# Attention and two feed-forward layers on one core: float32 products for the first pair of heads, one product for the last keys, and a new order

## The chip, the core and the metric

The kernel runs on one core of a Trainium2 chip. The core has five engines that run their own queues in order and wait for each other by semaphores: TensorE (PE in the profile; PEld is its loading of weights), VectorE (DVE), ScalarE (ACT), GpSimd (POOL) and SyncE (SP), which here only issues transfers. The metric is the device time of one execution in microseconds; lower is better. The kernel before took 784.59 us (median of three runs, 783.3 to 784.87).

## The reference, cut to what matters

Rotated attention over 2 batches of 8 heads, 576 tokens and 64 numbers a head; then a layer of four experts, all of which see every token, weighted by given shares; then a second feed-forward layer with a leaky rectifier.

```python
q_rot, k_rot = (rotate(q), rotate(k))       # x1*cos - x2*sin, x1*sin + x2*cos
scores = scale * np.matmul(q_rot, k_rot.transpose(0, 1, 3, 2))
scores = scores - np.max(scores, axis=-1, keepdims=True)
attn = np.exp(scores)
attn = attn / (np.sum(attn, axis=-1, keepdims=True) + 1e-09)
x = np.matmul(attn, v)                      # -> 1152 tokens x 512
...
for e in range(E):                          # 4 experts, 512 -> 1024 -> 512
    h = np.maximum(x @ w1[e], 0.0)
    out += p[:, e:e + 1] * (h @ w2[e])
...
h = x @ w_in                                # 512 -> 2048 -> 512
g = np.maximum(0.01 * h, h)
return g @ w_out
```

## The kernel before

Everything is float32 in and out. Most products are made of parts: a number is split into hi (rounded to the type fp32r) and lo (the rest), and a product becomes two to four products of parts. A split takes one instruction that rounds (`rounded`, on ScalarE or GpSimd) and one that subtracts.

**Attention** goes over eight pairs of heads, p = 0 to 7. For each pair q and k come in transposed, 128 rows (64 of either head) by 576 columns. They are rotated (`rope_mul` twice, `rope_add`; the names `x{p}_1` for k, `x{p}_0` for q), split (`x_hi`, `x_lo`) and stacked by transfers (`stk`), so that hi and lo of one head stand above each other. A pair has nine tiles of scores, numbered s0 to s71 over the whole kernel: four query blocks of 128 for each head, and one tile for the last 64 queries of both heads (576 = 4 x 128 + 64), whose weights lie in a block-diagonal tile `bd`. For each tile TensorE multiplies (`s_scores`), VectorE takes the negative maximum (`s_max`, tile `nm`), ScalarE the exponential (`s_exp`, tile `p`), TensorE turns the probabilities (`t_turn`, tile `t`), ScalarE and VectorE split what was turned (`t_hi`, `t_lo`, tile `pt`), and TensorE sums with v (`v_sum`, tile `o`). The keys are cut the same way; the last 64 keys of both heads share one tile of `pt`, and the tile `VZ` holds their v with zeros in the other head's rows. `v_sum` so takes ten products: four key tiles and the last keys, for lo and for hi of the probabilities. For pair 0 the split parts aren't stacked by transfers: q is copied into a zeroed `stk` (`first_zero`, `first_q`) and a tile of scores takes eight products of 288 columns; a later tile of 128 queries takes four.

**A part of the first layer lies in the attention.** As soon as the 512 tokens of block 0 are known (pairs 0 to 3), the three first half-experts are run for them in six steps v = 0 to 5 (`half_1`, tile `hp`; `half_2`, tile `hy`; VectorE's `half_relu` and `half_acc`): 288 products of 512 columns between the attention of pairs 4 to 7.

**The layers** then go over twelve units u of 512 hidden columns (eight of the first layer, four of the second) and three token blocks. For each unit the weights are loaded and split (`add_split`): in the first layer by GpSimd alone (L513 rounds, L517 subtracts, tiles `w` from `raw`), in the second, whose weights are 64-bit, by eight steps over VectorE, ScalarE and GpSimd (`split64`). `stage1` (L557, tile `ph`) and `stage2` (tile `py`) multiply.

**The order** of all this is made by a list planner (`Plan`): every task has engines that it may run on with a planned duration, tasks that it waits for, and a rank; the free engine takes the ready task of lowest rank. Ranks of the attention come from the tables `RANK` (three numbers a kind: first pair, pairs 1 to 3, pairs 4 to 7) and `MORE` (a penalty for the second engine). The planner fixes the order of every engine's queue; on the chip only semaphores decide when an instruction starts. Ahead of it, `WARM` products of the identity run on TensorE.

## Time and profile before

| | us |
|---|---|
| median of the runs | 784.59 |
| the profiled execution | 783.88 |
| its span, first to last instruction | 781.7 |
| TensorE busy | 756.2 (97%) |
| VectorE busy | 430.4 (55%) |
| GpSimd busy | 410.7 (53%) |
| ScalarE busy | 301.9 (39%) |

The shares are means over stages that differ. The span has four stretches: the start up to the first maximum, pairs 0 to 3, pairs 4 to 7 with the half-experts between them, and the layers. In each of them another engine can set the pace, so the rows below are read by stretch. "Granted clock" is the share of TensorE's full clock that the chip granted; 1.00 is the level of 2.4 GHz and 0.50 that of 1.2 GHz.

### The profile page before, as it was taken

The numbers are of one execution on the slowest core, as the hardware profiler recorded it, in microseconds if no ns is written. First come the engines' busy times: TensorE is split into PE (matmuls) and PEld (weight loads), VectorE is DVE, ScalarE is ACT, GpSimd is POOL, SyncE is SP. The second block draws the span as 40 slices with busy tenths as digits, with TensorE's granted clock in tenths as the row PEclk, the third lists the DMA queues.
The fourth block names the chain that finished last, engine by engine and source line by source line (L and its number), as shares of the span: only waits on it lengthen the run. The fifth ranks groups of instructions, "written<-read, shape, count | busy, mean of one in ns | idle before, by whom it ended". The sixth has DMA issues, their size and how long they took to land.

```text
span 781.7 us, 11049 instructions
## 1 busy us (share of the span) xinstructions
PE 756.2 (97%) x4204; PEld 667.0 (85%) x4204; DVE 430.4 (55%) x689; ACT 301.9 (39%) x686; POOL 410.7 (53%) x431
## 2 busy tenths in 40 slices
PE   6789899999999999999999999999999999999998
PEld 6778778888888989898898988988888889898897
DVE  7998977788752222232224222277668777762222
ACT  5688885766541111110112101143255454551221
POOL 7777857665339973433215331253157777782221
PEclk9999999999999999999999999999999999999999
DMA  7766545543053431320023100122113231000011
GB/s 254 184 194 158 148 109 141 169 118 100 24 220 108 136 104 37 102 55 30 25 54 105 58 28 28 54 84 80 55 55 107 61 103 55 0 1 1 1 55 67
DMA packets 31843, 67.70 MB, mean 87 GB/s; under 512 B 3888, under 2 KB 8752, under 8 KB 31792
## 3 DMA queue, kind: packets, MB, share of 16 engines
q1 hardware_dynamic: 30976, 66.22, 28.6%
q10 hardware_dynamic: 816, 0.79, 0.3%
q8 instruction: 33, 0.54, 0.3%
q14 instruction: 18, 0.15, 0.1%
HBM read 52.25 MB, written 2.36 MB: 70 GB/s over the span
## 4 chain that ended last, share of the span: by engine, by line
PE 84%; POOL 6%; DVE 5%; issue 2%; ACT 2%; DMA 1%; SPq 0%; POOLq 0%; DVEq 0%; ACTq 0%
PE py L463 33%; PE ph L557 32%; PE hp L660 4%; PE o L463 4%; PE hy L463 4%; PE s L303 4%; PE t L386 2%; POOL x L220 1%; DVE pt L415 1%; POOL x L223 1%; DVE nm L320 1%; DMA tab<-in_rope_dram 1%; DVE t L528 1%; ACT p L330 1%; POOL hw L653 1%
## 5 line engine op out<-in xcount | busy, mean ns | idle before, releaser
L557 PE MATMUL ph<-xT,w 128*128 128x256 f32 (+2 forms) x1584 | 276.0, 333 | 3.1 <-POOL w L517 1.6
L557 PEld LDWEIGHTS ph<-xT,w 128*128 128x128 f32 x1584 | 253.6, 190 | 23.0 <-POOL w L517 2.4
L463 PE MATMUL py<-w,h 128*128 128x512 f32 (+1 forms) x1164 | 268.0, 388 | 0.0
L463 PEld LDWEIGHTS py<-w,h 128*128 128x128 f32 x1164 | 215.8, 188 | 43.5
L564 ACT ACTIVATE h<-ph 128x384 fp32r<-128x384 f32 (+2 forms) x84 | 40.0, 476 | 249.2 <-PE ph L557 249.2
L568 DVE SCALAR_TENSOR_TENSOR h<-ph,h 128x384 fp32r<-128x384 f32 (+2 forms) x84 | 45.1, 537 | 114.3 <-ACT h L564 114.3
L513 POOL TENSOR_SCALAR w<-raw 128x512 fp32r<-128x512 f32 x64 | 38.5, 621 | 131.0 <-PE py L463 78.1
L603 DVE SCALAR_TENSOR_TENSOR acc<-py,prob,acc 128x512 f32<-128x512 f32 x55 | 41.2, 749 | 85.4 <-PE py L463 85.4
L582 POOL TENSOR_TENSOR h<-g,h 128x512 fp32r<-128x512 f32 (+2 forms) x48 | 52.1, 1086 | 63.4 <-ACT h L580 45.4
L517 POOL TENSOR_TENSOR w<-raw,w 128x512 fp32r<-128x512 f32 x64 | 81.2, 1291 | 0.0
L546 POOL TENSOR_TENSOR w<-t,w 128x512 fp32r<-128x512 f32 x32 | 44.5, 1403 | 53.2 <-ACT w L543 53.1
L415 DVE TENSOR_TENSOR pt<-t,pt 128x384 fp32r<-128x384 f32 (+2 forms) x128 | 60.0, 490 | 8.6 <-ACT pt L411 7.1
L303 PE MATMUL s<-stk 128*128 128x288 f32 x288 | 55.1, 323 | 8.9 <-ACT p L330 5.4
L411 ACT ACTIVATE pt<-t 128x384 fp32r<-128x384 f32 (+2 forms) x128 | 53.4, 439 | 24.2 <-PE t L386 20.8
L537 POOL TENSOR_TENSOR t<-t,r 128x512 int32<-128x512 int32 x32 | 44.4, 1388 | 26.2 <-DVE t L530 22.7
L330 ACT ACTIVATE p<-s,nm 128x576 f32<-128x576 f32 x72 | 53.2, 740 | 12.5 <-DVE nm L320 11.9
L320 DVE TENSOR_REDUCE nm<-s 128x1 f32<-128x576 f32 x72 | 53.6, 747 | 4.5 <-PE s L303 3.5
L303 PEld LDWEIGHTS s<-stk 128*128 128x128 f32 x288 | 43.6, 201 | 13.1 <-ACT p L330 7.8
L386 PE MATMUL t<-ident,p 128*128 128x128 f32 x288 | 46.2, 279 | 7.7 <-ACT p L330 3.4
L386 PEld LDWEIGHTS t<-ident,p 128*128 128x128 f32 x288 | 35.1, 142 | 14.3 <-ACT p L330 4.4
L463 PE MATMUL o<-pt,vs 128*128 128x320 f32 (+1 forms) x256 | 44.9, 302 | 0.1
L578 DVE TENSOR_TENSOR g<-ph,g 128x512 f32<-128x512 f32 (+2 forms) x48 | 26.4, 553 | 33.1 <-ACT g L576 33.1
(97 smaller groups left out, 837.5 us busy)
## 6 DMA issues: line engine op xcount, KB each, us to landing
raw<-in_w_dram SPq DMA_DIRECT2D x32, 512.0 KB, 3.7
raw<-in_w_in_dram SPq DMA_DIRECT2D x16, 512.0 KB, 3.8
raw<-in_w_out_dram SPq DMA_DIRECT2D x16, 512.0 KB, 3.6
x<-in_xqk_dram SPq DMA_DIRECT2D x14, 576.0 KB, 7.0
stk<-hl SPq DMA_DIRECT2D x28, 288.0 KB, 5.4
hraw<-in_w_dram SPq DMA_DIRECT2D x12, 512.0 KB, 3.8
stk<-hl SPq DMA_DIRECT2D x28, 144.0 KB, 3.3
v<-in_vp_dram SPq DMA_DIRECT2D x8, 288.0 KB, 4.7
```

Source lines behind the costliest of these rows:

```text
L303: pe.matmul(sc[:, c, :HS], lhsT=l, rhs=r[:, c * HS:(c + 1) * HS], start=(k == 0), stop=(k == len(ops) - 1))
L320: dve.tensor_reduce(out=NM[n], in_=SC[n][:, :, :HS], axis=AX.XY, op=ALU.max, negate=True)
L330: act.activation(PP[p, i][:, h].rearrange("p (c k) -> p c k", c=2), SC[n][:, :, :HS], AF.Exp, bias=NM[n], accum_out=SM[p][:, col:col + 1])
L386: pe.transpose(t[:, j], flat[:, b * P:(b + 1) * P], ident)
L411: act.activation(hi, src, AF.Copy)
L415: dve.tensor_tensor(out=lo, in0=src, in1=f32(hi), op=ALU.subtract)
L463: pe.matmul(ps, lhsT=l, rhs=r, start=(k == 0), stop=(k == len(ops) - 1))
L517: pool.tensor_tensor(out=w[:, 1], in0=raw, in1=f32(w[:, 0]), op=ALU.subtract)
L546: pool.tensor_tensor(out=w[:, 1], in0=f32(t), in1=f32(w[:, 0]), op=ALU.subtract)
L557: pe.matmul(ps, lhsT=w[:, c, l, fs], rhs=x[:, r, c], start=(c, k) == (0, 0), stop=(c, k) == (NC - 1, 2))
L568: dve.scalar_tensor_tensor(out=lo, in0=ps, scalar=0.0, in1=f32(hi), op0=ALU.max, op1=ALU.subtract)
L582: pool.tensor_tensor(out=lo, in0=g, in1=f32(hi), op=ALU.subtract)
```

## The change

- **First pair.** Its scores are made of two float32 products of 288 columns a tile; the parts, `x_hi`, `x_lo` and `first_q` are gone. The rotation of pair 0 runs on VectorE alone, with the scale in the product of q (`scalar_tensor_tensor`), and its sum writes straight into `stk` (`first_add`, for q one a head). The last queries of pair 0 use the tile `rr`.
- **Warm-up** of 28 products in place of 22. `fold` is gone: `r_rows` takes two float32 products with halves of the identity in place of one.
- **Last keys** of pairs 4 to 7 (`stacked`): for each head hi stands above lo in one block, so `v_sum` takes nine products in place of ten. For that the middle one of three turned tiles is split in three pieces (`t_hi`, `t_lo`: 256 columns, and twice 64 rows by 128).
- **First split** (unit 0): each rounding may go to ScalarE and each subtraction to VectorE.
- **Order**: other ranks for the first pair and for pairs 4 to 7 (the middle numbers stay), longer planned durations of `split64` and a rank 0.45 later, and a planned transfer rate of the first loads.

```diff
-WARM = 22
+WARM = 28
-RANK = {"tab_q": [2043.63, 1989.1, 2043.63], "zero": [1293.68, 1391.39, 1354.79], ...
+RANK = {"tab_q": [1899.26, 1989.1, 1475.09], "zero": [1519.84, 1391.39, 1696.99], ...
...
     def rope_mul(e, p, w, i, cs):
+        x = X[p, w][:, i, cs]
+        if p or w:
+            eng[e].tensor_tensor(out=x, in0=x, in1=(tab if w else tab_q)[:, i, cs], op=ALU.mult)
+        else:
+            dve.scalar_tensor_tensor(out=x, in0=x, scalar=SCALE, in1=tab[:, i, cs], op0=ALU.mult, op1=ALU.mult)
...
+    def first_k(cs=slice(0, S)):
+        return f32(stk_of(0)[:, 0, 1, cs])
+
+    def first_add(e, w, h, cs):
+        r = slice(64 * h, 64 * h + 64) if w == 0 else slice(0, P)
+        out = first_k(cs) if w else f32(stk_of(0)[r, h, 0, cs])
+        eng[e].tensor_tensor(out=out, in0=X[0, w][r, 0, cs], in1=X[0, w][r, 1, cs], op=ALU.add)
...
-        if p == 0 and i < KT:
-            ops = [(stk[:, h, a, at:at + P], k_of[b]) for a, b in ((1, 1), (0, 1), (1, 0), (0, 0))]
+        if p == 0:
+            ops = [(f32(stk[:, h, 0, at:at + P]) if i < KT else rr, first_k())]
...
-            pe.matmul(RB[p, c][:, 2 * P:], lhsT=rr, rhs=fold, start=True, stop=True)
+            products(RB[p, c][:, 2 * P:], [(rr, ident[:, :64]), (rr, ident[:, 64:])])
...
+        if i < KT and u == 1 and stacked(p):
+            if k == 0:
+                to, src = pt[:, :, 3:6:2, at:at + P], t[:, 0:3:2]
+            else:
+
+                h = k - 1
+                return pt[upper, h, KT, at:at + P], pt[lower, h, KT, at:at + P], t[64 * h:64 * h + 64, 1]
...
-            ops.append((VZ[p % 2][:, h].rearrange("p a d -> p (a d)"), pt[:, part, KT]))
+            if part == 0 or not stacked(p):
+                ops.append((VZ[p % 2][:, h].rearrange("p a d -> p (a d)"), pt[:, h if stacked(p) else part, KT]))
...
-                hi = plan.add(lambda e, c=c: split_hi(u, which, c), [("POOL", 0.6, 0)], loaded[c // 2:c // 2 + 1] + waits, rank + .1 * c)
+                hi = plan.add(lambda e, c=c: split_hi(e, u, which, c), [("POOL", 0.6, 0)] + [("ACT", 0.6, 0)] * (u == 0), loaded[c // 2:c // 2 + 1] + waits, rank + .1 * c)
...
-            for k, (e, us) in enumerate((("DVE", 0.4), ("DVE", 0.6), ("ACT", 0.55), ("ACT", 0.55), ("POOL", 1.2), ("DVE", 0.6), ("ACT", 0.5), ("POOL", 1.2))):
+            for k, (e, us) in enumerate((("DVE", 0.85), ("DVE", 1.0), ("ACT", 0.65), ("ACT", 0.65), ("POOL", 1.4), ("DVE", 1.0), ("ACT", 0.62), ("POOL", 1.38))):
...
-            split[u, which] = add_split(plan, u, which, loads, waits, rank, cv)
+            split[u, which] = add_split(plan, u, which, loads, waits, rank + (0.45 if u >= 2 * E else 0), cv)
```

What stands in the queues now, at three places. First VectorE at the start, up to the first maximum. Before (`x0_1` is k of pair 0, `x0_0` its q):

```order
L220 TENSOR_TENSOR x0_1_164<-x0_1_164,tab_132 128x288
L223 TENSOR_TENSOR x0_1_164<-x0_1_164 128x288
L244 TENSOR_TENSOR stk0_180<-x0_1_164,stk0_180 128x288
L220 TENSOR_TENSOR x0_1_164<-x0_1_164,tab_132 128x288
L220 TENSOR_TENSOR x0_0_178<-x0_0_178,tab_132 128x192
L223 TENSOR_TENSOR x0_1_164<-x0_1_164 128x288
L246 SCALAR_TENSOR_TENSOR hl0_208<-x0_0_178,hl0_208 128x192
L244 TENSOR_TENSOR stk0_180<-x0_1_164,stk0_180 128x288
L220 TENSOR_TENSOR x0_0_178<-x0_0_178,tab_132 128x384
L316 CAST bd0_135<-hl0_208 64x2x64
L220 TENSOR_TENSOR x0_0_178<-x0_0_178,tab_132 128x384
L320 TENSOR_REDUCE nm0_241<-s0_219 128x1
```

and after:

```order
L219 TENSOR_TENSOR x0_1_169<-x0_1_169,tab_131 128x288 x2
L234 TENSOR_TENSOR stk0_183<-x0_1_169 128x288
L219 TENSOR_TENSOR x0_1_169<-x0_1_169,tab_131 128x288
L221 SCALAR_TENSOR_TENSOR x0_0_181<-x0_0_181,tab_131 128x192 x2
L219 TENSOR_TENSOR x0_1_169<-x0_1_169,tab_131 128x288
L234 TENSOR_TENSOR stk0_183<-x0_0_181 64x192
L234 TENSOR_TENSOR stk0_183<-x0_1_169 128x288
L234 TENSOR_TENSOR stk0_183<-x0_0_181 64x192
L221 SCALAR_TENSOR_TENSOR x0_0_181<-x0_0_181,tab_131 128x384 x2
L335 TENSOR_REDUCE nm0_226<-s0_211 128x1
```

The three engines' chain of products, sum, rounding and subtraction has become products and sums on one engine; the copies into `bd` and the subtractions are gone from it.

Second, TensorE within pair 4, behind tile s40. Before (`hp` are products of the half-experts, `s` scores, `t` turns):

```order
L303 MATMUL s40_1516<-stk4_1202 128x288 x4
L660 MATMUL hp0_0_1524<-xT0_72,hw0_0_244 128x512 x3
L392 MATMUL t4_4_0_1532<-ident_64,p4_4_1501 128x64 x4
L393 MATMUL t4_4_0_1532<-ident_64,p4_4_1501 64x64
L660 MATMUL hp0_0_1524<-xT0_72,hw0_0_244 128x512 x3
L660 MATMUL hp0_1_1549<-xT0_72,hw0_0_244 128x512 x3
L392 MATMUL t4_4_1_1558<-ident_64,p4_4_1501 128x64 x4
L393 MATMUL t4_4_1_1558<-ident_64,p4_4_1501 64x64
L660 MATMUL hp0_0_1524<-xT0_72,hw0_0_244 128x512 x3
L386 MATMUL t4_1_0_1578<-ident_64,p4_1_1521 128x128 x3
```

and after:

```order
L319 MATMUL s40_1460<-stk4_1140 128x288 x4
L687 MATMUL hp0_0_1472<-xT0_71,hw0_0_217 128x512 x3
L407 MATMUL t4_4_0_1478<-ident_64,p4_4_1445 128x64 x4
L408 MATMUL t4_4_0_1478<-ident_64,p4_4_1445 64x64
L687 MATMUL hp0_0_1472<-xT0_71,hw0_0_217 128x512 x3
L407 MATMUL t4_4_1_1494<-ident_64,p4_4_1445 128x64 x4
L408 MATMUL t4_4_1_1494<-ident_64,p4_4_1445 64x64
L319 MATMUL s41_1503<-stk4_1140 128x288 x4
L687 MATMUL hp0_0_1472<-xT0_71,hw0_0_217 128x512 x3
L401 MATMUL t4_1_0_1520<-ident_64,p4_1_1484 128x128 x3
```

The next tile of scores stands ahead of products of the half-experts. Counted over the whole queue from s36 to s63 (pairs 4 to 6), 168 of the 288 products of the half-experts stood there before, and 120 now; the other 48 have gone behind s63. From s18 to s35 the order of TensorE is the same as before.

Third, where the layers begin: the split of unit 0 (`w0_0`), behind the last sum of the attention. GpSimd before:

```order
L458 TENSOR_TENSOR xT2_74<-xf7_1_2970,xT2_74 128x192
L513 TENSOR_SCALAR w0_0_3077<-raw0_0_0_3061 128x512 x2
L517 TENSOR_TENSOR w0_0_3077<-raw0_0_0_3061,w0_0_3077 128x512 x2
L513 TENSOR_SCALAR w0_0_3077<-raw0_0_1_3063 128x512 x2
L517 TENSOR_TENSOR w0_0_3077<-raw0_0_1_3063,w0_0_3077 128x512 x2
```

VectorE after, behind the last sum of the half-experts (two of the four subtractions; GpSimd keeps the other two and one rounding, ScalarE has three roundings):

```order
L712 SCALAR_TENSOR_TENSOR acc3_1841<-hy5_3_2992,prob_69,acc3_1841 128x512
L544 TENSOR_TENSOR w0_0_3063<-raw0_0_0_3047,w0_0_3063 128x512
L544 TENSOR_TENSOR w0_0_3063<-raw0_0_1_3049,w0_0_3063 128x512
```

The eight instructions of the split that were one queue are three queues now; VectorE's two stand behind `acc3`, which waits for the last product of the attention stage.

## Rows read from the trace of the kernel before

**Rows 1.** The page's first part: busy us, share of the span, instructions.

```profile
PE 756.2 (97%) x4204; PEld 667.0 (85%) x4204; DVE 430.4 (55%) x689; ACT 301.9 (39%) x686; POOL 410.7 (53%) x431
```

**Rows 2.** Busy time by stretch: stretch, length, engines, PEclk, DMA share, GB/s.

```profile
13.77:103.82 90.05, 76.96 (x540) 68.70 (x539) 81.41 (x156) 70.26 (x185) 72.06 (x79) 0.96 0.63 170
103.82:191.26 87.44, 86.52 (x547) 76.06 (x547) 67.72 (x123) 57.63 (x147) 56.23 (x69) 1.00 0.46 125
235.00:250.00 15.00, 13.23 (x59) 11.55 (x58) 4.00 (x7) 1.47 (x3) 15.00 (x18) 0.89 0.32 106
250.00:560.00 310.00, 310.00 (x1619) 273.91 (x1618) 111.97 (x168) 55.28 (x110) 126.95 (x131) 1.00 0.22 67
```

**Rows 3.** Timeline of the start, and s36's maximum: start, us, instruction, idle before it.

```profile
1.56 6.70 PE L698 MATMUL warm<-ident 128*128 128x128 f32 x44 [1.56 <-POOL ident masks.py:199]
4.75 0.46 DVE L220 TENSOR_TENSOR x<-x,tab 128x288 f32<-128x288 f32 x1 [0.39 <-DMA tab<-in_rope_dram]
...
7.48 1.33 DVE L220 TENSOR_TENSOR x<-x,tab 128x288 f32<-128x288 f32 x2 [0.16 <-DMA tab<-in_rope_dram]
...
11.53 3.89 PE L303 MATMUL s<-stk 128*128 128x288 f32 x16 [3.27 <-POOL vz L276]
...
13.77 0.76 DVE L320 TENSOR_REDUCE nm<-s 128x1 f32<-128x576 f32 x1
...
103.82 1.41 DVE L320 TENSOR_REDUCE nm<-s 128x1 f32<-128x576 f32 x2
```

**Rows 4.** Groups by shape: count | busy us, mean ns of one | idle before, releaser.

```profile
L246 DVE SCALAR_TENSOR_TENSOR hl<-x,hl 128x384 fp32r<-128x384 f32 x1 | 0.8, 819 | 0.0
...
L312 DVE CAST stk<-hl 64x768 fp32r<-64x768 f32 x1 | 0.9, 855 | 0.0
...
L316 DVE CAST bd<-hl 64x128 fp32r<-64x128 f32 x8 | 5.8, 731 | 0.1
...
L220 DVE TENSOR_TENSOR x<-x,tab_q 128x576 f32<-128x576 f32 x6 | 8.0, 1339 | 1.6 <-DMA x<-in_xqk_dram 1.6
...
L244 DVE TENSOR_TENSOR hl<-x,hl 128x576 fp32r<-128x576 f32 x7 | 6.9, 979 | 0.9 <-ACT hl L259 0.9
...
L223 DVE TENSOR_TENSOR x<-x 128x576 f32<-128x576 f32 x2 | 2.0, 994 | 0.1
...
L340 DVE TENSOR_SCALAR sm<-sm 128x4 f32<-128x4 f32 x3 | 1.7, 550 | 0.5 <-ACT p L330 0.5
...
L415 DVE TENSOR_TENSOR pt<-t,pt 128x384 fp32r<-128x384 f32 x96 | 51.0, 549 | 6.5 <-ACT pt L411 5.1
...
L415 DVE TENSOR_TENSOR pt<-t,pt 128x256 fp32r<-128x256 f32 x16 | 6.6, 415 | 2.0 <-ACT pt L411 1.9
...
L415 DVE TENSOR_TENSOR pt<-t,pt 64x64 fp32r<-64x64 f32 x16 | 3.4, 211 | 0.1
```

**Rows 5.** Chain that ended last, two pieces in pairs 4 to 7: start, us, work.

```profile
119.39 2.92 PE o L463 x20
...
230.63 2.40 PE o L463 x20
```

**Rows 6.** Timeline where the layers begin.

```profile
238.56 2.08 PE L557 MATMUL ph<-xT,w 128*128 128x384 f32 x8
...
238.76 0.75 DVE L685 SCALAR_TENSOR_TENSOR acc<-hy,prob,acc 128x512 f32<-128x512 f32 x1 [0.61 <-PE hy L463]
...
243.06 14.00 PE L557 MATMUL ph<-xT,w 128*128 128x384 f32 x85 [0.44 <-POOL w L517]
```

**Rows 7.** Groups by shape of two subtractions' kind, 128x512 (columns as in Rows 4).

```profile
L517 POOL TENSOR_TENSOR w<-raw,w 128x512 fp32r<-128x512 f32 x64 | 81.2, 1291 | 0.0
...
L540 DVE SCALAR_TENSOR_TENSOR t<-sq,t 128x512 f32<-128x512 f32 x32 | 33.3, 1045 | 8.9 <-POOL t L537 8.9
```

**Rows 8.** Timeline where the second layer begins.

```profile
596.30 1.66 DVE L530 SCALAR_TENSOR_TENSOR t<-raw,t 128x512 int32<-128x512 int32 x1
...
598.49 2.35 PE L557 MATMUL ph<-xT,w 128*128 128x384 f32 x12 [1.38 <-DVE g L578]
```

139 lines of the change are left out of this document (73 added, 66 removed), and 6 rows, old and new, of the table RANK.

## Prediction, made before the result was known

> **What bounds the kernel now.** I read the shares of the span first, then the same busy times by stretch, then the timeline at the seams and the chain of waits in pairs 4 to 7. TensorE is busy 97% of the span and VectorE 55% [rows 1], so over the whole only about 25 us of TensorE's idle time can be won, and only where it lies. By stretch: from 250 to 560 us TensorE is busy 310.00 of 310 us at clock 1.00 [rows 2]; nothing there gets shorter, since the change takes no product out of the layers. In pairs 0 to 3 (13.77 to 103.82) VectorE is busy 81.41 of 90.05 us, a share of 90.4%, and TensorE 76.96: VectorE sets the pace. In pairs 4 to 6 (103.82 to 191.26) it is the other way round: TensorE 86.52 of 87.44, idle 0.92, and VectorE at 77% [rows 2]. So a change is worth what it takes from VectorE in the first four pairs, and what it takes from TensorE in the next ones. Besides there are three seams where TensorE stands: the start [rows 3], the begin of the layers [rows 6] and the second layer [rows 8].
>
> I make the sum against the profiled run, 783.88 us; the median of the runs, 784.59, lies 0.7 above it, and I add that at the end.
>
> **A. The first maximum comes earlier: -2.0 us** (bounds -1.0 and -2.3). Now it starts at 13.77. VectorE began the second half of the rotation at 7.48, when the table had landed, and TensorE ran the first 16 products from 11.53, in 3.89 us, after a lull of 3.27 [rows 3]. After the change VectorE's queue is its own chain. The first half of k (two products and a sum, 0.46 each as the row at 4.75) ends near 6.1 and is covered by the wait for the table. From 7.48: one 288-column product 0.46, two of 192 columns 0.80, the other product 0.46, two sums of 64x192 some 0.4 each with the 0.46 of k between or after them; the first tile can start near 10.1. It has two float32 products of 288 columns. The trace has no such product; it has the warm-up's 22 float32 products of 128 columns, which stand as 44 records and take 6.70 us, 0.15 a record [rows 3]. A product of 288 columns at the same rate a column is 2 x 0.15 x 288/128 = 0.68, so 1.4 a tile as upper bound; as lower bound two records a product as quick as the half-clock 288-column ones of the row at 11.53 (3.89/16 = 0.24), 0.96. Taken: 1.0, ready near 11.1. VectorE first has two scaled products of 384 columns in its queue (0.82 each at most, the row of 128x384 [rows 4]; 0.55 at least, the subtraction of that size), which end by then or 0.7 later. So the first maximum starts near 11.8, against 13.77. Six more warm products (0.30 each [rows 3]) end near 9.5 in place of 8.3 and hide in the wait; they shorten the lull to less than 1 us.
>
> **B. Pairs 0 to 3: -1.8 us** (0 to -2.1). VectorE sets this pace, and of pairs 1 to 3 the order has stayed. Gone from VectorE behind the first maximum [rows 4]: the 384-column subtraction 0.82, a copy of q into `stk` 0.86, a copy into `bd` 0.73, one 576-column product 1.34, one 576-column subtraction 0.98 (the order of after has one fewer of either there); sum 4.73. Added: two sums of 64x384 at 0.55 each (a 128x384 operation), two copies into `rr` at 0.21 (64x64), one 576-column sum 0.99, one small operation 0.55; sum 3.06. Net -1.67, and at a share of 90.4% (1.67/0.904) -1.85 us. Together A and B bring s36's maximum from 103.82 to 100.0.
>
> **C. Pairs 4 to 7: +0.6 us** (bounds -1.5 and +4.7). TensorE loses one of ten products in each of 16 sums: the sums now take 2.92 us for 20 products of 320 columns and 2.40 for 20 of 256 [rows 5], 0.146 and 0.120 each; 8 of either make -2.1. The second product in `r_rows` is a 64-column float32 one, which the trace doesn't show: from 0 to 0.30 (a whole 128-column one); four at 0.15, +0.6. That is -1.5. VectorE pays for it: of 16 middle tiles the subtraction of 128x384 (0.549) becomes 0.415 and two of 64x128 (0.21 to 0.35; taken 0.28) [rows 4], 0.43 more each, 6.9 us over pairs 4 to 7; ScalarE gets about as many roundings more, beside other work. And the order moves 48 of the 288 products of the half-experts from between s36 and s63 to behind s63. One of 512 columns is 512/384 of a layer's product (14.00/85 = 0.165 [rows 6]), 0.22; so 10.6 us of TensorE's work leave this stretch. There TensorE then has 86.52 - 10.6 - 1.2 = 74.7 us, while VectorE, at 67.72 now, gains 5.2 of the split (twelve middle tiles) and loses four sums of the moved half-experts (0.75 each, the row at 238.76 [rows 6]) and two rectifiers (two 512-column operations each, 0.73 by scaling 0.549 from 384 columns), and so keeps 67.0. At the 90.4% which it reached where it set the pace, that takes 67.0/0.904 = 74.1. The two are level, so TensorE will wait for VectorE here and there: no less than the 0.92 now, and no more than 9.6% of 74, 7.1. I take 3.0, 2.1 above now: -1.5 + 2.1 = +0.6. Behind s63 the moved products cost what they cost before it.
>
> **D. The begin of the layers: -2.4 us** (bounds +0.9 and -4.4). The last sum of the attention stage ends at 238.56 (T). The next 12 products of 384 columns would take 12 x 0.165 = 2.0 us; they end at 243.06 + 0.165, so TensorE stands 2.7 us for GpSimd's chain of eight [rows 6]. In the 15 us from 235 the granted clock is 0.89, which is 0.11 x 15 = 1.65 us lost [rows 2]. After, two of four subtractions are on VectorE behind `acc3`, which ends at T + 0.95 [rows 6]. For a 128x512 subtraction there I take the one row of that size, 1.045 [rows 7] (0.73 by the scaling in C). Two of them and the four products behind: T + 0.95 + 2.1 + 0.2 + 0.7 = T + 3.9; the stall is 1.9, a gain of 0.8. With the shorter stop I take the lost clock as kept too: at the start a lull of 3.27 us stood before the slow products [rows 3], and here none is left that long.
> GpSimd's and VectorE's subtractions lie beside each other in this place. GpSimd's of that size is 1.291 on the mean of 64, VectorE's 1.045 on the mean of 32 where scaling gives 0.73 [rows 7]: some slowing is in the rows, full turns are not. The Trainium skill ("SBUF — State Buffer", section "Who interferes with whom") says that a VectorE instruction with two SBUF inputs and a GpSimd instruction exclude each other; the trace agrees in part, and by it nothing would be gained here, the rival P below.
>
> **E. The second layer: -1.4 us** (0 to -1.4). There TensorE waits 1.38 us for `g`, with a split step of 1.66 us ahead of it on VectorE [rows 8]. With the later rank one split step stands between the two operations of `g` in question where three stood. The cover that is gone is the weights' lead: they come later by two steps, but the next unit is tens of microseconds away.
>
> The other edits (tables, `bd` and `rr` zeroing, the transfers' planned rate, the wider `v` load) have work beside them: TensorE's first product waits for VectorE, and the shares of the transfers are 0.63 and less [rows 2]. Nothing.
>
> **Sum**: -2.0 - 1.8 + 0.6 - 2.4 - 1.4 = -7.0; 783.88 - 7.0 = 776.9, and 0.7 more for the median: **777.6 us**.
>
> **Rivals.** *F, TensorE stays fed in pairs 4 to 6*: C is -1.5 in place of +0.6, 775.5. For it: the two engines are level by the sum, and ranks put scores earlier. Against: three queues in a ring seldom run at 100% both. *P, the two subtractions hold each other up*: VectorE's and GpSimd's take turns, and the last ends at T + 0.65 + 1.29 + 0.73 + 1.29 + 0.73 = T + 4.7, the products 0.9 behind it, T + 5.6; the stall is 3.6 and the clock isn't kept: D is +0.9 in place of -2.4, 780.9. For it: 1.291 and 1.045 are both long for their size. Against: neither row shows a stop. *B0, the early start is given back*: a transfer or GpSimd's `v` parts in pairs 0 to 3 come last, and s36 starts at 103.8 as now: A and B are 0, 781.4. The change then doesn't reach where it aims. For it: GpSimd is busy 72.06 of 90.05 us there [rows 2]. Against: VectorE's 90.4% leaves others little to hold up. P and B0 together give 784.7, no change. *V, slower: VectorE becomes the pace of pairs 4 to 6*. Each middle tile now makes three roundings and three subtractions in turn before its sum, so the path from maximum to sum is longer and VectorE waits within it. At a share of 76%, about as now (67.72/87.44 = 77% [rows 2]), its 67.0 us take 88.2 and not the 77.7 that the forecast has (74.7 and the 3.0 idle); 10.5 more, 788.1. It decides against the change from a share below 79%, where 67.0 us take 84.8, 7 more than forecast. Against it: that share is low now because TensorE is full, and was 90.4% where VectorE set the pace.
>
> **How the numbers follow.** The forecast 0.45, F 0.12, P 0.18, B0 0.10, P with B0 0.06, V 0.09. Within 0.2%, 1.6 us, is about what a measurement of this kernel can't tell from no change: faster 0.85, same 0.06, slower 0.09. The range reaches from 774.0 (F, with A and D at their better ends) to 782.5 (P and B0 alone, with C 1 us worse); it leaves out V and P with B0, and a little at the low end.
>
> **What would show it.** A: the first maximum at about 11.8, its tile's two products 1.0 us before. B: s36's maximum near 100. C: in pairs 4 to 6 TensorE idle some 3 us and VectorE's share near 90%; sums of 18 products and 2.63 and 2.16 us. D: the first 12 products of the layers over 3.9 us behind the last sum, VectorE's subtraction there 0.7 to 1.05, the clock 1.00. E: no wait for `g` near 590. Wrong it would be by VectorE idle in pairs 4 to 6 at a share under 80%, by a clock under 1.00 in the first pair's float32 products or the layers' first ones, or by a subtraction of over 2 us where the layers begin.

## The result, and the profile after

The changed kernel is slower. It took 790.36 us (median of four runs), the kernel before 783.94 beside it; the ratio is 1.0082, with a 95% interval of 1.0062 to 1.0102. Forecast were 777.6 us and a range of 774.0 to 782.5. The profiled execution of after took 787.1 us with a span of 785.3.

The page of after, first part (it answers to [rows 1]), busy us, share of the span and instructions:

```profile
PE 755.4 (96%) x4180; PEld 662.2 (84%) x4180; DVE 449.1 (57%) x726; ACT 308.8 (39%) x718; POOL 397.1 (51%) x406
```

TensorE has as much to do as before; VectorE is busy 18.7 us longer. Busy time by stretch of after, the columns as in [rows 2]; the stretches run between the first, the 37th and the 64th maximum, the last product of the attention stage and the first product of the second unit of the layers:

```profile
12.65:103.08 90.43, 75.58 (x512) 65.53 (x512) 83.24 (x158) 69.54 (x184) 70.00 (x76) 0.94 0.65 174
103.08:186.32 83.24, 75.32 (x476) 64.57 (x476) 73.25 (x135) 56.92 (x159) 46.88 (x58) 0.98 0.47 119
186.32:246.49 60.17, 60.17 (x348) 51.86 (x347) 41.48 (x80) 32.66 (x86) 25.52 (x34) 1.00 0.31 106
246.49:277.22 30.73, 28.95 (x170) 26.88 (x169) 13.29 (x18) 5.22 (x12) 27.51 (x27) 1.00 0.52 172
```

The last two of these stretches in the kernel before, which [rows 2] cut in another way:

```profile
191.26:238.72 47.46, 47.46 (x285) 41.42 (x284) 32.20 (x61) 23.74 (x60) 19.58 (x30) 1.00 0.31 111
238.72:271.36 32.64, 30.87 (x170) 28.39 (x169) 8.04 (x14) 4.48 (x10) 32.64 (x37) 0.95 0.46 143
```

From the two profiles, after less before, step by step of the forecast:

| step | forecast | measured |
|---|---|---|
| A, start to the first maximum | -2.0 | 12.65 - 13.77 = -1.1 |
| B, first to 37th maximum | -1.8 | 90.43 - 90.05 = +0.4 |
| C, 37th maximum to the end of the attention stage | +0.6 | (83.24 + 60.17) - (87.44 + 47.46) = +8.5 |
| D, begin of the layers | -2.4 | 30.73 - 32.64 = -1.9 |
| E, the rest, with the second layer | -1.4 | (785.3 - 277.2) - (781.7 - 271.4) = -2.2 |
| sum | -7.0 | +3.7 |

The two seams of the layers came within 0.8 us of the forecast. The loss is C, and nearly all of it lies in one place. Between the 37th and the 64th maximum TensorE is idle 83.24 - 75.32 = 7.9 us, where it was 0.9, and 4.7 us of that is one hole. Timeline of after around it, all engines, in order of time:

```profile
137.32 1.29 POOL L274 TENSOR_TENSOR vs<-v,vs 128x512 fp32r<-128x512 f32 x1
...
138.23 5.65 DVE L355 TENSOR_SCALAR sm<-sm 128x5 f32<-128x5 f32 x1
...
138.58 0.61 POOL L267 TENSOR_SCALAR hw<-hraw 128x512 fp32r<-128x512 f32 x1
...
138.89 1.55 PE L687 MATMUL hp<-xT,hw 128*128 128x512 f32 x6
...
139.17 2.51 POOL L680 TENSOR_TENSOR hw<-hraw,hw 128x512 fp32r<-128x512 f32 x2
141.64 0.86 POOL L484 TENSOR_TENSOR xT<-xf,xT 128x64 fp32r<-128x64 f32 x2
...
142.46 1.39 POOL L219 TENSOR_TENSOR x<-x,tab_q 128x576 f32<-128x576 f32 x1
143.79 0.74 DVE L335 TENSOR_REDUCE nm<-s 128x1 f32<-128x576 f32 x1
...
145.15 0.74 PE L401 MATMUL t<-ident,p 128*128 128x128 f32 x3 [4.71 <-DVE pt L440]
```

The second row is the addition of 1e-9 to five sums of the softmax. It is among the smallest instructions that VectorE has here (one on four sums takes 0.17 us at 36.80), and it takes 5.65 us. GpSimd runs seven instructions from 137.32 to 143.85 without a pause, and the addition ends at 143.88, with the last of them. Behind it in VectorE's queue stand the maxima and subtractions for which TensorE waits. VectorE's row counts as busy all that time, so a share of busy time shows nothing of it; the duration does, against the shape. Behind the hole the granted clock falls: its mean in the stretch is 0.98, and 0.02 x 83.24 is 1.7 us.

In the first pair, too, VectorE's instructions are long for their size. From the timeline of after (the third answers to the maximum at 13.77 of [rows 3]):

```profile
10.62 2.11 DVE L221 SCALAR_TENSOR_TENSOR x<-x,tab 128x384 f32<-128x384 f32 x2
...
10.85 1.47 POOL L274 TENSOR_TENSOR vs<-v,vs 128x512 fp32r<-128x512 f32 x1
...
12.65 0.74 DVE L335 TENSOR_REDUCE nm<-s 128x1 f32<-128x576 f32 x1
...
16.55 1.71 DVE L331 COPY rr<-stk 64x64 f32<-64x64 f32 x2
...
16.82 1.39 POOL L219 TENSOR_TENSOR x<-x,tab 128x576 f32<-128x576 f32 x1
...
18.41 2.26 PE L319 MATMUL s<-stk,rr 128*128 128x288 f32 x4 [3.54 <-DVE rr L331]
```

The two products of 384 columns take 2.11 us; the first maximum, whose scores were ready near 11.1 (two tiles take TensorE 2.18 us from 9.98), starts when they end. Two copies of 64x64 take 1.71 us beside GpSimd's product, and TensorE stands 3.54 us for the second.

So the theory, **H**: a VectorE instruction that has to share something with GpSimd is held while GpSimd runs, and what it costs depends on what GpSimd does in that moment and on who waits behind. Rivals: the 5.65 us is an accident of one execution; or VectorE is simply full in pairs 4 to 6, with the three-piece split on the path, and the time is lost whatever the addition does.

### The profile page after: what moved, and what is told of

The parts are those of the page before. It is cut to its first block, busy times and chain, and to the rows that moved or that the text cites. A ratio compares the mean times of both kernels' runs of the same rounds, so it can differ in the third digit from the quotient of the medians.

```text
span 785.3 us, 11078 instructions
## 1 busy us (share of the span) xinstructions
PE 755.4 (96%) x4180; PEld 662.2 (84%) x4180; DVE 449.1 (57%) x726; ACT 308.8 (39%) x718; POOL 397.1 (51%) x406
## 4 chain that ended last, share of the span: by engine, by line
PE 88%; DVE 6%; ACT 2%; issue 2%; DMA 1%; ACTq 0%; DVEq 0%
PE ph L584 34%; PE py L489 33%; PE s L319 4%; PE hp L687 4%; PE hy L489 4%; PE o L489 4%; PE t L401 3%; DVE pt L440 2%; DVE nm L335 1%; DMA x<-in_xqk_dram 1%; ACT p L345 1%; DVE hl L252 1%; ACT pt L436 1%; PE t L407 1%; PE tr L645 1%
## 5 line engine op out<-in xcount | busy, mean ns | idle before, releaser
L584 PE MATMUL ph<-xT,w 128*128 128x384 f32 (+2 forms) x1584 | 273.8, 331 | 1.8 <-DVE w L544 1.8
L267 POOL TENSOR_SCALAR w<-raw 128x512 fp32r<-128x512 f32 x57 | 35.5, 644 | 134.6 <-PE py L489 81.7
L544 POOL TENSOR_TENSOR w<-raw,w 128x512 fp32r<-128x512 f32 x60 | 77.3, 1314 | 0.0
L440 DVE TENSOR_TENSOR pt<-t,pt 128x384 fp32r<-128x384 f32 (+3 forms) x160 | 67.7, 437 | 9.1 <-ACT pt L436 6.9
L436 ACT ACTIVATE pt<-t 128x384 fp32r<-128x384 f32 (+3 forms) x160 | 57.7, 395 | 30.6 <-PE t L401 26.0
L319 PE MATMUL s<-stk 128*128 128x288 f32 x256 | 52.4, 332 | 3.9 <-ACT p L345 3.6
L319 PEld LDWEIGHTS s<-stk 128*128 128x128 f32 x256 | 39.1, 195 | 8.8 <-ACT p L345 5.8
L603 ACT ACTIVATE g<-ph 128x512 f32<-128x512 f32 (+2 forms) x48 | 23.4, 487 | 56.2 <-PE ph L584 54.8
```

What stands on the lines that cost most here:

```text
L319: pe.matmul(sc[:, c, :HS], lhsT=l, rhs=r[:, c * HS:(c + 1) * HS], start=(k == 0), stop=(k == len(ops) - 1))
L436: act.activation(hi, src, AF.Copy)
L440: dve.tensor_tensor(out=lo, in0=src, in1=f32(hi), op=ALU.subtract)
L544: eng[e].tensor_tensor(out=w[:, 1], in0=raw, in1=f32(w[:, 0]), op=ALU.subtract)
L584: pe.matmul(ps, lhsT=w[:, c, l, fs], rhs=x[:, r, c], start=(c, k) == (0, 0), stop=(c, k) == (NC - 1, 2))
```

## The experiments

A run's time stands beside that of the kernel before on the same chip; medians of the latter were 783.2 to 784.5, and 785.0 from one single run.

**The same kernel again.** No edit.

> The changed kernel itself once more, with a second profile. The profile of the changed kernel has one hole of 4.71 us on TensorE at 140.44 in pair 5, behind a 128x5 addition of 1e-9 on VectorE that took 5.65 us while GpSimd ran six instructions in a row. Theory H (VectorE is held by GpSimd, and where this falls changes little from run to run, since the order is fixed): the same addition takes about 5.6 us again, and the median stays at 790 us. Rival R1 (a chance event of that one execution): the addition takes under 1.5 us and TensorE's idle time between the 37th and the 64th maximum is 8.0 - 4.7 = 3.3 us; but since that profiled execution was the fastest of four (787.1), the others then lost their time elsewhere, and the median stays too, with other holes.

790.08 us, ratio 1.0086 (1.0063 to 1.0108). In the second profile the same addition takes 5.63 us and the hole is 4.68. It is no accident. The stretch from the 37th to the 64th maximum, second profile:

```profile
102.97:187.69 84.72, 76.78 (x476) 65.42 (x476) 73.23 (x136) 56.83 (x159) 46.81 (x58) 0.96 0.46 117
```

It is 1.5 us longer than in the first profile with the same idle time: the mean clock is 0.96 here and 0.98 there. What follows the hole differs from execution to execution.

**Without the additions.** Each sum holds the exponential of zero and so is at least 1; adding 1e-9 leaves it as it is in float32.

```diff
         if e == "ACT":
-            act.activation(sums(p, c), sums(p, c), AF.Copy, bias=1e-9)
+            pass
         else:
-            dve.tensor_scalar_add(sums(p, c), sums(p, c), 1e-9)
+            pass
```

> The changed kernel without the sixteen additions of 1e-9 to the sums of the softmax (each sum is at least 1, so the addition leaves float32 as it is); the order of all engines else as it was. Theory H (that addition, held by GpSimd for 5.4 us, opens the hole in pair 5): no hole over 2 us in pairs 4 to 6, TensorE's idle time there 8.0 - 4.7 = 3.3 us, the granted clock not falling at 145, the whole 5 to 6 us less than the changed kernel: 784 to 785.5. Rival R2 (VectorE is simply full there, the path through the three-piece split is what lasts): only the additions' own 0.2 us each go, 789 to 790, and holes of the same sum stand elsewhere.

777.36 us, ratio 0.9945 (0.9922 to 0.9969): 12.7 us less than the changed kernel, more than theory H had asked for. By stretch:

```profile
11.88:99.73 87.85, 76.21 (x514) 66.85 (x512) 80.37 (x152) 70.02 (x183) 72.32 (x77) 0.94 0.68 183
99.73:176.40 76.67, 73.37 (x476) 63.69 (x476) 67.30 (x132) 56.46 (x157) 46.82 (x58) 1.00 0.51 129
99.73:236.56 136.83, 133.53 (x822) 115.54 (x822) 107.67 (x211) 88.76 (x240) 72.32 (x91) 1.00 0.41 119
```

The second line is what the forecast had said of pairs 4 to 6: VectorE 67.30 us (forecast 67.0), TensorE idle 3.3 (3.0), the length 76.67 (77.7). Ahead of the 37th maximum (99.73, not 103.08) another 3.3 us are gone; there six additions of 0.17 to 1.06 us stood on VectorE, 3.0 in sum. Single profiles don't size that part well: further down, a run with all the additions in place has this maximum at 101.18, where the changed kernel's two profiles have 103.08 and 102.97.

**Pairs 4 to 7 as before**, all else changed: the old third numbers of `RANK`, ten products in a sum, whole splits.

```diff
...
-        return p >= NPAIR
+        return False
...
-                    mid = big and u == 1 and p >= NPAIR
+                    mid = False
```

> The changed kernel with pairs 4 to 7 as before: the old ranks there, the last keys in ten products, no three-piece split. First pair, begin of the layers and second layer stay changed. Theory H and R2 alike: pairs 4 to 7 cost what they cost before, 8.5 us less than in the changed kernel's profile; 783.9 - 0.7 (36 maxima) - 1.9 (begin of the layers) - 2.2 (second layer) = 779.1. If it stays above 784, the loss does not lie in pairs 4 to 7 and my reading of the two traces by stretch is wrong.

782.62 us, ratio 1.0000 (0.9975 to 1.0025). The profiled execution, the fastest of ten, took 779.86, near the forecast, the median is 3.5 us over it. The loss lies in pairs 4 to 7, as the traces say.

**New order without the stacked keys**: the same edit, with the new ranks kept.

> The changed kernel with its new ranks, but without the stacked last keys: ten products in a sum, whole splits. Theory R2 (the three-piece split, 6.9 us more on VectorE and as many on ScalarE, opens the holes): TensorE's 2.1 us come back, the holes go, 784 to 786. Rival R3 (the new order alone opens them: 48 products of the half-experts moved behind the 64th maximum leave TensorE with nothing to put between): idle time in pairs 4 to 6 stays at 5 to 8 us, 790 to 792.

783.82 us, ratio 0.9996 (0.9984 to 1.0009). This looked like the proof that the three-piece split is to blame. It isn't. In the orders of this run and of the one ahead of it the planner gives the addition of pair 5's first chunk to ScalarE, where it takes 0.20 and 0.21 us. Both edits so removed the hold together with what they were to test; the run without additions, in which the split is untouched, tells the two apart.

**The control: the kernel before without its additions.**

> The kernel before without the sixteen additions of 1e-9. Theory H (what an addition costs is how long GpSimd holds it, and who waits behind): in the trace of before none was held over 1.06 us; three of 0.64 to 1.06 lie in pairs 1 to 3, where VectorE sets the pace, one in pair 6, where TensorE is full. So 1 to 2.5 us less: 781 to 782.5. Rival R4 (the additions cost the same in any order, some 13 us as in the changed kernel): 771 to 774.

782.65 us, ratio 0.9982 (0.9969 to 0.9996). The same sixteen instructions that cost the changed kernel 12.7 us cost the kernel before 0.7.

**Another form in the same place.** The additions on VectorE become reductions over one element, which write each sum back as it is.

```diff
-            dve.tensor_scalar_add(sums(p, c), sums(p, c), 1e-9)
+            dve.tensor_reduce(out=sums(p, c), in_=sums(p, c).unsqueeze(2), axis=AX.X, op=ALU.add)
```

> The changed kernel with each VectorE addition of 1e-9 replaced by a reduction over one element in the same place of the same queue (it writes the sum back as it is, which is what the addition gives too, since the sums are at least 1). Theory H (it is the form of the instruction that GpSimd holds up): the reduction takes 0.15 to 0.3 us wherever it stands, no hole of 4.7 us in pair 5, the whole as without the additions, 777 to 779. Rival R5 (whatever stands in that place of VectorE's queue waits until GpSimd stops, or the sums come late): the instruction takes over 5 us again, 789 to 791.

780.10 us, ratio 0.9948 (0.9924 to 0.9972). The group by shape (columns as in [rows 4]):

```profile
L355 DVE TENSOR_REDUCE sm<-sm 128x4 f32<-128x4 f32 x5 | 0.8, 157 | 0.2 <-ACT p L345 0.2
L355 DVE TENSOR_REDUCE sm<-sm 128x5 f32<-128x5 f32 x5 | 0.8, 154 | 0.0
```

Ten instructions of 0.15 to 0.16 us, the one in pair 5 among them, and no hole. So it is neither the place in the queue nor late sums; it is the form. (The median is 2.7 us over the run without additions. Its profile starts 1.6 us later at the first maximum and has a stretch of half clock where the layers begin; the reductions themselves are 1.6 us in all.)

**One addition alone.** Fifteen are left out, the one of pair 5, first chunk, is kept.

```diff
...
-            dve.tensor_scalar_add(sums(p, c), sums(p, c), 1e-9)
+            if (p, c) == (5, 0):
+                dve.tensor_scalar_add(sums(p, c), sums(p, c), 1e-9)
```

> The changed kernel with fifteen of the sixteen additions of 1e-9 left out, and only the one of pair 5, first chunk, kept: the instruction that took 5.65 and 5.63 us in the two profiles of the changed kernel. Theory H (this one, held by GpSimd, makes the hole): it takes over 5 us again, the hole of 4.7 us and a stretch of half clock behind it return, 777.4 + 4.6 + 1.7 to 3.4 = 783.7 to 785.4. Rival R8 (it depends on what runs in the microsecond in which it falls, and without the others it falls elsewhere): it takes under 1.5 us, 777 to 779.

785.22 us, ratio 1.0028 (1.0013 to 1.0044), 7.9 over the run with none. The group of the addition, TensorE's first row behind it, and the stretch from the 37th to the 64th maximum, three views of this run:

```profile
L356 DVE TENSOR_SCALAR sm<-sm 128x5 f32<-128x5 f32 x1 | 5.6, 5629 | 0.0
```

```profile
141.61 0.88 PE L402 MATMUL t<-ident,p 128*128 128x128 f32 x3 [4.68 <-DVE pt L441]
```

```profile
99.52:183.93 84.41, 76.37 (x476) 65.38 (x476) 72.27 (x134) 56.54 (x157) 46.79 (x58) 0.96 0.47 117
```

One instruction of five numbers a partition makes this stretch 84.41 - 76.67 = 7.7 us longer: 4.7 us are the hole, and 3.0 are longer busy time of TensorE at a mean clock of 0.96 (0.04 x 84.41 = 3.4).

**Why six instructions and not one.** In pairs 1 to 3 an addition was held by one GpSimd instruction (1.06 us at most). Three changes of the run with one addition. First, a reduction ahead of it, so that it comes 0.15 us later:

```diff
             if (p, c) == (5, 0):
+                dve.tensor_reduce(out=sums(p, c), in_=sums(p, c).unsqueeze(2), axis=AX.X, op=ALU.add)
```

> As the run with one addition kept, with a reduction over one element (0.15 us) ahead of that addition in VectorE's queue, so that it begins 0.15 us later beside the same row of GpSimd. There it passed by six changes from one GpSimd instruction to the next, though in pairs 1 to 3 such an addition got in at the first. Theory S (it is a matter of the moment at which it comes): it gets in at one of the first changes, 0.2 to 1.5 us, and the hole is gone. Rival S2 (GpSimd's row there lets nothing of this form in): 5.3 to 5.6 us again.

788.34 us in a single run; the addition takes 5.46 us. Second, the addition as a `tensor_tensor` maximum of the sums with themselves, the same values:

```diff
-                dve.tensor_scalar_add(sums(p, c), sums(p, c), 1e-9)
+                dve.tensor_tensor(out=sums(p, c), in0=sums(p, c), in1=sums(p, c), op=ALU.max)
```

> As the run with one addition kept, but the addition is a tensor_tensor maximum of the sums with themselves: the same values, two inputs in SBUF. In the trace of the changed kernel VectorE's instructions with two such inputs waited for one GpSimd instruction (1.0 to 2.0 us for 576 columns), none for a row of six. Theory F (only the one-input forms tensor_scalar, copy and cast are passed by): 0.2 to 1.5 us. Rival F2 (any form that GpSimd holds would wait there to the end of its row): over 5 us.

783.82 us in a single run; 5.62 us. A start 0.15 us later changed nothing, and neither did another form of those that are held. Third, GpSimd's two subtractions in that row in the other order:

```diff
+        if (v, which) == (1, 1):
+            j = 1 - j
         hi, lo, raw = half_parts(v, which, j)
         pool.tensor_tensor(out=lo, in0=raw, in1=f32(hi), op=ALU.subtract)
```

> As the run with one addition kept, with GpSimd's two subtractions of the half-expert's weights in that row in the other order: the first one now needs what GpSimd's instruction just ahead of it writes, so GpSimd has to wait for itself there once; before, all six found what they needed ready. Theory G (VectorE gets in where GpSimd has to wait, were it for its own last instruction, and is passed by where GpSimd's next instruction is ready): the addition ends about 139.2 in place of 140.3 or later, 0.9 to 1.1 us long, the hole is gone. Rival G2 (such a wait makes no opening): 5.4 to 5.7 us again.

778.04 us in a single run, the hole gone. GpSimd and VectorE in that place, then the group of the addition:

```profile
134.69 1.28 POOL L274 TENSOR_TENSOR vs<-v,vs 128x512 fp32r<-128x512 f32 x1
135.94 0.62 POOL L267 TENSOR_SCALAR hw<-hraw 128x512 fp32r<-128x512 f32 x1
136.63 2.53 POOL L683 TENSOR_TENSOR hw<-hraw,hw 128x512 fp32r<-128x512 f32 x2
...
135.60 0.98 DVE L356 TENSOR_SCALAR sm<-sm 128x5 f32<-128x5 f32 x1
136.49 0.74 DVE L335 TENSOR_REDUCE nm<-s 128x1 f32<-128x576 f32 x1
```

```profile
L356 DVE TENSOR_SCALAR sm<-sm 128x5 f32<-128x5 f32 x1 | 1.0, 978 | 0.0
```

GpSimd's instruction at 135.94 ends at 136.56 and the next starts at 136.63, since it needs what the one ahead writes. In the changed kernel the next one started at 139.17, 0.02 us ahead of the end of its forerunner. In that opening of 0.07 us VectorE got in, as theory G had it. (GpSimd's ends are rough in a profile; what shows the point is that the swap removes the hold, and not the 0.07.)

**The changed kernel with that swap alone**, all additions kept.

> The changed kernel complete, with all its additions, and only the two subtractions of the half-expert's weights in pair 5 in the other order. Theory G: the addition there takes about 1 us, the hole of 4.7 us and the 3.4 to 6.8 us of half clock behind it go, which is 8 us of the 37th to 64th maximum; from 790.1: 780 to 783, faster than before or the same. If it stays over 787, the hole of that place isn't what makes the changed kernel slower.

780.97 us, ratio 0.9968 (0.9945 to 0.9990): the order of two GpSimd instructions turns 0.8% slower into 0.3% faster. The addition takes 0.99 us there. From the 37th to the 64th maximum:

```profile
101.18:178.34 77.16, 73.79 (x476) 63.53 (x476) 68.79 (x135) 56.88 (x159) 47.00 (x58) 1.00 0.51 128
```

**What the change of pairs 4 to 7 is worth without the hold**: the edit of the third run, and no additions.

> The changed kernel without the additions and with pairs 4 to 7 as before (old ranks there, ten products in a sum, whole splits). It shows what the change of pairs 4 to 7 is worth when no addition is held. Forecast (step C): the change costs 0.6, so 777.4 - 0.6 = 776.8. Rival R9 (with the hold gone the stacked last keys pay, 1.5 us and more): 779 to 780, as the run with old pairs 4 to 7 and the additions (782.6) less the 2.5 us that these took in pairs 1 to 3.

780.41 us, ratio 0.9972 (0.9952 to 0.9992): 3.0 over the run that has the change, though the two intervals overlap. The stage from the 37th maximum on, in this run and in the control (the kernel before without its additions):

```profile
100.27:239.76 139.49, 136.18 (x838) 118.03 (x838) 100.03 (x179) 85.46 (x210) 73.25 (x96) 1.00 0.41 117
```

```profile
101.34:237.96 136.62, 134.20 (x830) 117.47 (x830) 99.92 (x179) 80.25 (x201) 75.76 (x99) 1.00 0.42 119
```

The run with the change has 136.83: 2.7 less than this run, but 0.2 more than the control. With the old ranks the planner, which starts from another first pair, does not give back the order of the kernel before either: between the 37th and the 64th maximum lie 132 products of the half-experts here and in the third run, 171 in the kernel before, 120 in the changed one. So this run doesn't show that the change pays; against the control, one profile each, it is worth nothing, near the 0.6 that I had booked as its cost.

**The first pair.** Two runs take away holds there. One makes VectorE's copies into `bd` and `rr` as reductions over one element, without additions:

```diff
-            eng[e].tensor_copy(rr[r, r], f32(STK[0][r, h, 0, cs]))
+            copy_of(e, rr[r, r], f32(STK[0][r, h, 0, cs]))
...
+        if e == "DVE":
+            dve.tensor_reduce(out=out, in_=x.unsqueeze(len(x.shape)), axis=AX.X, op=ALU.max)
```

> The changed kernel without the additions, and VectorE's copies into the block-diagonal tiles (two of 64x64 into rr, six of 64x128 into bd) made as a reduction over one element. In the run without the additions the copies of pair 1 took 1.33 and 1.25 us and one of pair 4 1.31, where 0.28 is the least. Theory H (a copy is a form that GpSimd holds, a reduction isn't): each copy takes 0.2 to 0.35, the 37th maximum comes 1 to 2 us earlier, 775.5 to 776.5. Rival R7 (the next instruction with two inputs in SBUF is held in its place): same as without, 777 to 778.

776.18 us, ratio 0.9910 (0.9875 to 0.9945), faster than both kernels, with nothing left out of the result. The copies take 0.21 to 0.28 us. But the 37th maximum comes at 99.09, 0.6 us ahead of the run without additions, where 1 to 2 were expected, and the 1.2 us between the medians lie within the scatter of the two runs (773.9 to 780.1 and 777.1 to 780.8). The other run, on top of that, puts fillings in the place of GpSimd's early subtractions, five of them (the expectation counts six); the lo parts of these are missing from its result:

```diff
+        if v == 0:
+            pool.memset(f32(lo), 0.0)
+            return
         pool.tensor_tensor(out=lo, in0=raw, in1=f32(hi), op=ALU.subtract)
...
+        if p == 0:
+            pool.memset(f32(VS[p][:, :, 1, :]), 0.0)
+            return
```

> The kernel of the run with copies as reductions, in which GpSimd's subtractions for the first pair's v and for the first half-expert's weights (six of 128x512, 1.3 us each, most of them within the first 20 us) are fillings with zero of the same tiles; the lo parts of these are left out of the result so. VectorE's instructions and all orders stay. Theory H (VectorE's first-pair products and sums, with two inputs in SBUF, are held by GpSimd's reading there: 1.06, 0.67 and 1.07 us in that run): they take their least (0.57, 0.43 and 0.75), the 10th maximum comes 1.5 to 3 us earlier (38.35 there), 773.5 to 774.7. Rival R10 (these holds lie beside TensorE's own work): the same as there, 775.5 to 777.

771.79 us, ratio 0.9854 (0.9836 to 0.9872), 4.4 below the run ahead of it and better than either theory had it; its four executions lie within 1.6 us, those of the run ahead within 6.2. The same three VectorE instructions and the stretch up to the 37th maximum, first with the subtractions, then with the fillings:

```profile
10.22 2.11 DVE L221 SCALAR_TENSOR_TENSOR x<-x,tab 128x384 f32<-128x384 f32 x2
...
12.92 2.41 DVE L234 TENSOR_TENSOR stk<-x 64x384 f32<-64x384 f32 x2
...
16.63 1.81 DVE L219 TENSOR_TENSOR x<-x,tab 128x576 f32<-128x576 f32 x1
```

```profile
12.25:99.09 86.84, 75.48 (x515) 65.44 (x513) 76.95 (x152) 68.55 (x182) 71.06 (x76) 0.96 0.67 183
```

```profile
10.30 1.15 DVE L221 SCALAR_TENSOR_TENSOR x<-x,tab 128x384 f32<-128x384 f32 x2
...
12.04 1.74 DVE L234 TENSOR_TENSOR stk<-x 64x384 f32<-64x384 f32 x2
...
15.08 0.88 DVE L219 TENSOR_TENSOR x<-x,tab 128x576 f32<-128x576 f32 x1
```

```profile
11.38:96.16 84.78, 74.58 (x514) 64.02 (x512) 76.79 (x153) 68.93 (x183) 66.66 (x77) 0.98 0.71 192
```

These three rows are 2.6 us shorter in sum, and the 37th maximum comes 2.9 us earlier. A filling is also shorter than a subtraction (0.53 us against 1.3), so a part of the gain may be GpSimd's own time; this run doesn't part them.

**The same aim without leaving anything out**: the planner may split the first half-expert's weights only behind the first chunk of pair 0.

```diff
+                hold0 = [t for k in [(0, 0)] for t in written.get(k, [])]
...
-                    hi = task("half_hi", v, lambda e, v=v, which=which, j=j: half_hi(e, v, which, j), one(512, "POOL", "ACT"), [t_l] + w_w)
+                    hi = task("half_hi", v, lambda e, v=v, which=which, j=j: half_hi(e, v, which, j), one(512, "POOL", "ACT"), [t_l] + w_w + (hold0 if v == 0 else []))
```

> The kernel of the run with copies as reductions, in which the planner may split the first half-expert's weights only once the first chunk of pair 0 is split, so that GpSimd's reading instructions leave the first 20 us; nothing is left out. The order of the other queues moves a little. Theory H (a part of the 4.4 us that the run with fillings gained is to be had so): 772 to 775. Rival R11 (GpSimd's work comes later in pairs 0 to 3, where it is 80% busy, and holds VectorE there, or delays pair 1): 776 to 779.

793.63 us, ratio 1.0126 (1.0098 to 1.0153), worse than all. The planner gave copies to GpSimd and placed much else anew; pairs 0 to 3 now last 96.22 us, with new holes. The first of them, on TensorE, and what VectorE and GpSimd did ahead of it:

```profile
36.62 0.41 PE L386 MATMUL rb<-ident,rw 128*128 128x128 f32 x2 [3.72 <-DVE xf L470]
```

```profile
31.19 3.44 DVE L722 TENSOR_SCALAR psum_e<-psum_e 128x9 f32<-128x9 f32 x1
```

```profile
30.95 1.19 POOL L267 TENSOR_SCALAR hw<-hraw 128x512 fp32r<-128x512 f32 x2
32.12 2.48 POOL L686 TENSOR_TENSOR hw<-hraw,hw 128x512 fp32r<-128x512 f32 x2
34.57 1.39 POOL L219 TENSOR_TENSOR x<-x,tab_q 128x576 f32<-128x576 f32 x1
```

This is the same hold in a second place. The addition of 1e-9 to the sums of the experts' shares, 128x9, takes 0.17 us in eleven of the other profiles and 0.65 to 1.00 in six; here it stands 3.44 us, through three changes from one GpSimd instruction to the next, and ends with the second subtraction. The sum for which TensorE waits stands behind it in VectorE's queue.

**The first pair as before**, all else changed, no additions.

```diff
-WARM = 28
+WARM = 22
...
-        if p == 0:
-            ops = [(f32(stk[:, h, 0, at:at + P]) if i < KT else rr, first_k())]
+        if p == 0 and i < KT:
+            ops = [(stk[:, h, a, at:at + P], k_of[b]) for a, b in ((1, 1), (0, 1), (1, 0), (0, 0))]
```

> The changed kernel without the additions and with the first pair as before: its rotation over three engines, split parts, eight products a tile, the old ranks of the first pair and 22 warm-up products; all else (stacked last keys, ranks of pairs 4 to 7, first split, second layer) changed. It shows what the new first pair is worth. Forecast (steps A and B): 3.8 us, so 777.4 + 3.8 = 781.2. Rival R6 (the first pair's work, now on VectorE beside GpSimd, is held there as often as it saves): within 1 us of 777.4.

789.96 us, ratio 1.0082 (1.0063 to 1.0100). This one doesn't answer its question. The 37th maximum comes at 103.43, 3.7 us later than in the run without additions, which is what A and B had said; but the planner, given another first pair, placed the half-experts of pairs 4 to 7 differently too, and 8.9 us of the 12.6 lie behind that maximum. And in the control, which has the same first pair, the 37th maximum stands at 101.34. The seven profiles with the new first pair, its copies and subtractions as in the changed kernel, in which no addition was held before that maximum have it between 98.4 and 101.6, 100.3 in the middle. So the new first pair is worth some 1 to 3 us, in single profiles that scatter by as much.

## Why the prediction was wrong

**What bounds the kernel** was read rightly: from the second unit to the second layer the two kernels differ by 0.4 us in 317 (271.36 to 588.47 before, 277.22 to 593.94 after), and the gains and losses lie at the places named.

**A** failed by 0.9 us, on the two products of 384 columns: "0.82 each at most, 0.55 at least". They took 2.11 us together, the second 1.6, since GpSimd's subtraction for `vs` ran beside them. With fillings in the place of GpSimd's subtractions two of them take 1.15. The 0.82 that I called an upper bound was one row's duration, and one row bounds nothing that depends on a neighbour. The float32 products cost what was taken: 2.18 us for two tiles, against 1.0 a tile. How far the hold reaches there changes from run to run: in the run without additions the same second product took 0.68 us and the first maximum stands at 11.88, near the forecast. (The working also has the longer warm-up end near 9.5; 8.3 and six times 0.30 are 10.1, and it ended at 9.87. The sum doesn't hang on it.)

**B** failed by 2.2 us. The sum of what VectorE loses and gains was made with mean durations, and the means of the removed operations (0.73 for a copy, 1.34 for a 576-column product) are to a large part waiting: the same copy takes 0.27 as a reduction, the 576-column products of the kernel before take 0.74 to 0.76 in four cases of eight and 1.41 to 2.02 in the others. And a hold that is taken away need not come back as time: as reductions the two copies of pair 1 take 0.27 and 0.28 in place of 1.33 and 1.25, and the 37th maximum came 0.6 us earlier. That the next operation takes over the hold is my reading; no run shows it by itself. With GpSimd's early subtractions gone, the 37th maximum comes at 96.16, 3.8 us ahead of the forecast's 100.0; with them at 98.4 to 101.6, and with the additions too at 101.2 to 103.1 (three profiles).

**C** failed by 7.9 us, and this alone turned the sign. The step that failed isn't in the sum: the addition of 1e-9 was there before and after, 0.55 us in [rows 4] (B counts one of them at that), and in pairs 4 to 7 I counted nothing for it, because the diff doesn't touch its line. The new ranks do: in the kernel before VectorE has no such addition between 93.55 and 180.84 us (ScalarE has pair 5's), in the changed one it has, beside a row of seven GpSimd instructions. The queues of the two kernels would have shown the first half of that ahead of the run; I compared them at three places, and not for every instruction that changed its engine or its neighbours. Without the additions step C was right up to the 64th maximum (VectorE 67.30 us, idle 3.3), and 1.3 us off in sum, +1.9 against +0.6. TensorE's idle time rose by 2.4 (0.92 to 3.30), near the 2.1 taken; its busy time in the stage fell by 0.45 (133.98 to 133.53) where the working had 1.5. The sums with v gave what was reckoned (26.01 to 23.92 us, -2.1), the products of `r_rows` cost 1.0 more (3.74 to 4.74) and not 0.6; the rest isn't traced to one kind of product.

**D** came out at -1.9 against -2.4, by one of its two terms. The stop didn't get shorter: in the stretch behind the last product TensorE is idle 32.64 - 30.87 = 1.77 us before and 30.73 - 28.95 = 1.78 after, and the twelfth product of the layers starts 4.50 us behind the first before (243.06 [rows 6]) and 4.26 after, where 0.8 were counted as gain. What is gained is TensorE's busy time, 1.92 us: before, the clock is at half for 3.4 us from 243.7 on (mean 0.95), after, it stays at 1.00. That was the other term, 1.65. It isn't sure in each run: of the 16 profiles with the changed split three have half clock there too, and both with the old split have it. VectorE after, where the layers begin, with GpSimd and TensorE (it answers to [rows 6]):

```profile
247.20 5.41 DVE L544 TENSOR_TENSOR w<-raw,w 128x512 fp32r<-128x512 f32 x4
```

```profile
245.11 5.93 POOL L544 TENSOR_TENSOR w<-raw,w 128x512 fp32r<-128x512 f32 x4
```

```profile
248.27 0.79 PE L584 MATMUL ph<-xT,w 128*128 128x384 f32 x3 [0.89 <-DVE w L544]
249.95 3.24 PE L584 MATMUL ph<-xT,w 128*128 128x384 f32 x17 [0.90 <-DVE w L544]
```

VectorE's four subtractions average 1.35 us and GpSimd's 1.48, where GpSimd's alone took 1.291 [rows 7] and 1.045 was taken for VectorE's: each engine is slow beside the other, as rival P had it, but not by full turns, where a subtraction of either would take 1.29 + 0.73 us together. P's price came due in part: the twelfth product ends some 4.4 us behind the first one's start, between the forecast's 3.9 and P's 5.6. P counted the turns from 0.65 us behind that start; GpSimd had begun its first subtraction 1.2 us ahead of it.

**E** was right in its mechanism: the wait for `g` is gone. The same products across that seam, before and after:

```profile
588.47:632.30 43.83, 42.45 (x219) 36.90 (x218) 35.38 (x42) 22.07 (x44) 32.47 (x27) 1.00 0.31 96
```

```profile
593.94:635.94 42.00, 42.00 (x217) 36.80 (x216) 35.08 (x43) 22.38 (x45) 32.98 (x27) 1.00 0.32 100
```

That is 1.8 us, of which 1.4 are the idle time; the bound of 1.4 was exceeded.

Of the **rivals**, P had the right mechanism in the wrong place. It was priced for two subtractions, where the diff puts both engines on one task, and not for VectorE's other instructions beside GpSimd's other work, whose order the change had moved everywhere. V had the right place and nearly the measured time, 788.1, by a wrong mechanism: VectorE is at 73.25/83.24 = 88% there, not 76%, and 5.5 us of that are one instruction that stands; that the time came so near is luck. B0 came nearly true ahead of the 37th maximum (103.08 and 102.97, where it had 103.8) and named GpSimd's `v` parts for it; the run with fillings bears that out in part, by VectorE's instructions that are held and not by a late transfer. The Trainium skill ("SBUF — State Buffer", section "Who interferes with whom") was quoted for the two subtractions; the same section lists `copy`, `cast` and `tensor_scalar` among VectorE's forms that can contend with GpSimd, and says of `tensor_reduce` that on trn2 it never does. The runs agree with both lists (5.63 us as `tensor_scalar`, 0.15 as `tensor_reduce`). Where they differ is in how long: the section gives the shared ports to whichever issues first for its whole instruction, and here VectorE waited for a whole row of GpSimd's instructions.
